# A new division of PSUM in windowed attention, and five units masked on TensorE

## The chip, the cores and the metric

One core of a Trainium2 chip runs the whole program. The metric is the device time of one execution in microseconds (us). Executions of the same kernel within one set of rounds here spread by 0.3 to 1.1%. One program is profiled once, so profiles of two kernels are two single executions, and the medians come from several.

## The reference

```python
# attention: B, H, S, D = 8, 8, 576, 64, window 64
scores = q @ k.T / sqrt(D)
scores = where(0 <= i - j < 64, scores, -1e9)
x = softmax(scores) @ v                  # heads side by side: (4608, 512)
# mixture of experts: 8 experts, F = 1024, one per token
logits = x @ w_gate
fresh = argmax(logits)
e = fresh where s == 0 or sigmoid(x @ w_local) < 0.5, else the previous token's e
out = softmax(logits)[e] * (relu(x @ w1[e]) @ w2[e])
```

## The kernel before

Attention takes the 4608 tokens as 9 blocks of 512 and the 8 heads as 4 pairs, which gives 36 units of one block and one pair. TensorE computes scores two units ahead, ScalarE takes exp, VectorE multiplies by a 0/1 mask, TensorE multiplies by the values, VectorE divides. In between, blocks 0 to 3 have their x turned (transposed) for the gates, blocks 4 to 8 get gates from turned values that are loaded, and VectorE works the first part of the router during blocks 4 to 7. After attention come the experts.

The kernel divides PSUM, the memory that TensorE's products land in, into 8 banks of 512 fp32 per partition. Before, two double banks hold scores and two double banks hold everything else: values, turns, gates, logits and the router's products.

```python
ps_s = tile_pool(name="at_ps_s", bufs=2, space=PSUM)          # (cut: contexts)
ps_x = [tile_pool(name=f"at_ps_x{i}", bufs=1, space=PSUM) for i in range(2)]

def bank():
    ps_x.reverse()
    return ps_x[0].tile([P, 2, SC], F32, name="xo")

def turn(sc, x, half):
    r = bank()
    for i in range(2):
        for c in range(4):
            nc.tensor.transpose(r[:, i, ...], x[:, c, 2 * half + i], ident)
    o = pp.tile([P, 2, SC], F32, name="p")
    nc.scalar.copy(o, r)

def scores(sc, hp):
    sp = ps_s.tile([P, 2, SC], F32, name="sp")
    ...                                    # 18 products of 64x64 with 64x128 or 64x64 (36 records in the trace)
    nc.scalar.activation(p, sp, Act.Exp, scale=DH ** -0.5)
    nc.vector.tensor_tensor(p, p, mask, op=Alu.mult)

def values(sc, hp, p, x, g):
    xo = bank()
    ...                                    # 16 products (32 records), then VectorE reads xo

for i, (sc, hp) in enumerate(units):
    ps[units[i + LEAD]] = scores(*units[i + LEAD])
    ...
    for _ in range(2 if sc else 4):
        next(moves, None)                  # shift copies of the next block's values, on ScalarE and GpSimd
    ...                                    # a turn, gates, logits or a copy of gates (spread)
    values(sc, hp, ps.pop((sc, hp)), x, g)
```

A shift copy makes a part of vb, a second arrangement of the next block's values; the gates' copy (spread) puts the turned gates beside the values.

## Time and profile before

| | before |
|---|---|
| time, median of 4 runs | 663.25 us (660.32 to 664.8) |
| profiled execution, span | 661.9 us |
| end of the last values product | 139.36 us |
| from there to the end (experts) | 522.5 us |
| TensorE's waits on ScalarE's turn copies | 2.4 + 0.8 us |
| TensorE's waits on the gates' copy and the logits | 5.3 + 1.9 us |

### The profile page before, as it was taken

The numbers are of one execution on the slowest core, as the hardware profiler recorded it, in microseconds if no ns is written. First come the engines' busy times: TensorE is split into PE (matmuls) and PEld (weight loads), VectorE is DVE, ScalarE is ACT, GpSimd is POOL, SyncE is SP. The second block draws the span as 40 slices with busy tenths as digits, with TensorE's granted clock in tenths as the row PEclk, the third lists the DMA queues.
The fourth block names the chain that finished last, engine by engine and source line by source line (L and its number), as shares of the span: only waits on it lengthen the run. The fifth ranks groups of instructions, "written<-read, shape, count | busy, mean of one in ns | idle before, by whom it ended". The sixth has DMA issues, their size and how long they took to land. (4 is left out here: it accounts for less than half of the span.)

```text
span 661.9 us, 15065 instructions
## 1 busy us (share of the span) xinstructions
PE 630.8 (95%) x6521; PEld 545.4 (82%) x6521; DVE 385.4 (58%) x693; ACT 177.7 (27%) x274; POOL 122.3 (18%) x128
## 2 busy tenths in 40 slices
PE   7888878999999999999999999999999999999996
PEld 7766666787677799989989998999799979997984
DVE  7665589774941268368528844863666366537410
ACT  4755645521111121212212230322131213211200
POOL 4311112311204111122113111311211120101011
PEclk9999998999999999999999999999999999999998
DMA  9989989999878967487468657755865586457540
GB/s 339 417 326 352 330 298 371 401 348 358 324 286 331 352 221 280 168 331 277 161 237 356 226 223 278 294 201 178 313 243 192 189 310 244 162 192 284 207 156 23
DMA packets 22479, 178.37 MB, mean 269 GB/s; under 512 B 3037, under 2 KB 4195, under 8 KB 11652
## 3 DMA queue, kind: packets, MB, share of 16 engines
q1 hardware_dynamic: 13588, 147.82, 59.3%
q0 software_dynamic: 8816, 29.50, 11.3%
q8 instruction: 53, 0.87, 0.5%
q14 instruction: 22, 0.18, 0.1%
HBM read 158.43 MB, written 19.40 MB: 269 GB/s over the span
## 5 line engine op out<-in xcount | busy, mean ns | idle before, releaser
L1185 POOL DMA_INDIRECT out_dram<-y,idx x36 | 38.2, 1061 | 301.1 <-DVE y L1164 141.9
L1203 PEld LDWEIGHTS hp<-xt,w 128*128 128x128 f32 (+1 forms) x1152 | 88.3, 168 | 3.6 <-issue 3.2
L1203 PE MATMUL hp<-xt,w 128*128 128x128 f32 (+1 forms) x1152 | 89.7, 252 | 0.0
L1112 PE MATMUL hp<-xs,ws 128*128 128x128 f32 x624 | 73.9, 275 | 0.0
L1112 PEld LDWEIGHTS hp<-xs,ws 128*128 128x128 f32 x624 | 71.8, 192 | 0.0
L1155 PE MATMUL hp<-ws,hs 128*128 128x256 f32 x312 | 71.6, 379 | 0.0
L1234 PE MATMUL yp<-w,h 128*128 128x512 f32 x160 | 71.0, 594 | 0.2 <-issue 0.2
L1036 POOL DMA_INDIRECT xg<-xs,idx x40 | 46.5, 1164 | 116.3 <-PE tp L1061 85.8
L1155 PEld LDWEIGHTS hp<-ws,hs 128*128 128x128 f32 x312 | 59.3, 190 | 8.1
L354 DVE TENSOR_TENSOR p<-p,mask 128x1024 f32<-128x1024 f32 x36 | 47.4, 1320 | 20.5 <-ACT p L351 20.2
L1234 PEld LDWEIGHTS yp<-w,h 128*128 128x128 f32 x160 | 29.5, 190 | 32.9 <-issue 32.1
L1123 DVE TENSOR_TENSOR h<-hp,keep 128x512 f32<-128x512 f32 x39 | 26.9, 691 | 49.0 <-PE hp L1112 48.0
L364 PE MATMUL xo<-vb,p 128*64 128x74 f32 (+1 forms) x576 | 44.4, 229 | 10.2 <-DVE va L304 5.3
L364 PEld LDWEIGHTS xo<-vb,p 128*64 128x64 f32 x576 | 38.9, 138 | 18.4 <-issue 8.6
L1112 PEld LDWEIGHTS hp<-xt,w 128*128 128x128 f32 x416 | 49.3, 192 | 3.4 <-issue 2.4
L1164 DVE SCALAR_TENSOR_TENSOR y<-hp,pw,kept 128x256 f32<-128x256 f32 x39 | 18.3, 482 | 56.2 <-issue 33.6
L1112 PE MATMUL hp<-xt,w 128*128 128x128 f32 x416 | 51.0, 276 | 0.0
L351 ACT ACTIVATE p<-sp 128x1024 f32<-128x1024 f32 x36 | 36.8, 1026 | 48.0 <-PE sp L335 43.1
L1155 PE MATMUL hp<-w,h 128*128 128x256 f32 x208 | 49.5, 381 | 0.0
L335 PE MATMUL sp<-w 64*64 64x128 f32 (+1 forms) x1296 | 43.1, 269 | 3.3 <-issue 2.0
L335 PEld LDWEIGHTS sp<-w 64*64 64x64 f32 x1296 | 37.4, 137 | 10.2 <-issue 6.9
L364 PE MATMUL xo<-va,p 128*64 128x74 f32 (+1 forms) x576 | 44.6, 230 | 1.0 <-issue 1.0
(268 smaller groups left out, 898.8 us busy)
## 6 DMA issues: line engine op xcount, KB each, us to landing
w<-in_w_dram SPq DMA_DIRECT2D x54, 2048.0 KB, 8.4
w<-in_kq_dram SPq DMA_DIRECT2D x17, 1024.0 KB, 10.5
xs<-x POOLq DMA_DIRECT2D x9, 1024.0 KB, 12.7
va<-in_v_dram SPq DMA_DIRECT2D x5, 1184.0 KB
vtt<-in_vt_dram SPq DMA_DIRECT2D x5, 1024.0 KB, 7.1
va<-in_v_dram SPq DMA_DIRECT2D x3, 1040.0 KB, 11.5
va<-in_v_dram SPq DMA_DIRECT2D x2, 520.0 KB, 10.3
w<-in_kq_dram SPq DMA_DIRECT2D x2, 512.0 KB
```

Of the source, the lines that this page charges most:

```text
L335: nc.tensor.matmul(sp[c * WIN:(c + 1) * WIN, j, a:b], lhsT=kt[h, hp, block * WIN:(block + 1) * WIN], rhs=qt[h, hp, a:b], start=True, stop= ...
L351: nc.scalar.activation(p, sp, Act.Exp, scale=DH ** -0.5)
L354: masked.append(nc.vector.tensor_tensor(p, p, m.to_broadcast([P, 2, SC]), op=Alu.mult))
L364: nc.tensor.matmul(xo[par * WIN:(par + 1) * WIN, j, s * VW:s * VW + n], lhsT=p[:, j, b * WIN:(b + 1) * WIN], rhs=w[:, s, 2 * hp + j, :n], ...
L1036: self.nc.gpsimd.indirect_dma_start(out=x, out_offset=None, in_=self.xs[:rows, :], in_offset=bass.IndirectOffsetOnAxis(ap=idx[:, s:s + 1], ...
L1112: nc.tensor.matmul(out[:, m, :], lhsT=a[:, kk, m * P:(m + 1) * P], rhs=b[:, kk, :], start=start and m + kk == 0, stop=stop and (m, kk) == ...
L1123: nc.vector.tensor_tensor(o, x, y, op=add)
L1155: nc.tensor.matmul(out, lhsT=a[:, m, :], rhs=b[:, m, :], start=start and m == 0, stop=stop and m == FK // 2 - 1, skip_group_check=True)
L1164: nc.vector.scalar_tensor_tensor(y[i][:, j * w:(j + 1) * w], x, pw[i], y2, Alu.mult, Alu.add)
L1185: self.nc.gpsimd.indirect_dma_start(out=self.out[:, :], out_offset=bass.IndirectOffsetOnAxis(ap=st["idx"][:, s:s + 1], axis=0), in_=y, in_ ...
L1203: nc.tensor.matmul(hp[a, i, :], lhsT=st["w1"][:, kk, m * P:(m + 1) * P][:, a], rhs=st["xt"][:, kk, :n], start=(kk == 0), stop=(kk == DK - 1))
L1234: nc.tensor.matmul(yp, lhsT=st["h"][:, m, :P], rhs=st["w2"][:, m, :], start=(m == 0), stop=(m == FK - 1))
```

## The change

The intent is to let no values product wait for a bank that gates or router steps hold. Scores get three single banks (so exp runs in two halves), values keep two double banks for themselves, and one single bank serves everything else. Five units at the time of the router leave VectorE's mask out: before the scores, TensorE adds -1e30 where the mask is 0 (an identity times a bias tile), so exp gives 0 there.

```diff
-    ps_s = ctx.enter_context(tc.tile_pool(name="at_ps_s", bufs=2, space=PSUM))
-    ps_x = [ctx.enter_context(tc.tile_pool(name=f"at_ps_x{i}", bufs=1, space=PSUM)) for i in range(2)]
+    ps_s = ctx.enter_context(tc.tile_pool(name="at_ps_s", bufs=3, space=PSUM))
+    ps_e = ctx.enter_context(tc.tile_pool(name="at_ps_e", bufs=1, space=PSUM))
+    ps_x = ctx.enter_context(tc.tile_pool(name="at_ps_x", bufs=2, space=PSUM))
     def bank():
-        ps_x.reverse()
-        return ps_x[0].tile([P, 2, SC], F32, name="xo")
+        return ps_e.tile([P, SC], F32, name="r")
...
+BIASED = [(4, 3), (5, 1), (5, 3), (6, 1), (6, 3)]
+    def build_bias():
+        colf = columns()                     # an iota and a cast in a buffer of the pool of p
+        ...                                  # four tensor_scalar into bias, then unit and never
...
     def scores(sc, hp):
-        sp = ps_s.tile([P, 2, SC], F32, name="sp")
+        sp = [ps_s.tile([P, SC], F32, name="sp") for _ in range(2)]
+        if biased:
+            ...
+            nc.tensor.matmul(sp[j][c * WIN:(c + 1) * WIN, a], lhsT=unit[h], rhs=x, start=not n, stop=False, ...)
...
-        nc.scalar.activation(p, sp, Act.Exp, scale=DH ** -0.5)
+        for j in range(2):
+            nc.scalar.activation(p[:, j], sp[j], Act.Exp, scale=DH ** -0.5)
+        if biased:
+            return p
...
-            if hp == 0:
-                turn(sc - 1, old, 1)         # 8 transposes into a double bank
+            if hp == 0:
+                turn(sc - 1, old, 2)         # 4 transposes, before values
...
+            if hp == 0:
+                turn(sc - 1, old, 3)         # 4 transposes, after values
...
+        sums = tl("sums", P, 2 * E * CMAX)[:, :2 * n * E]
+        vec.tensor_copy(sums, both)          # the router empties the single bank at once
```

The cuts hold the gates for 64 columns ahead of block 4 (now apart), a rule that router steps keep off the single bank while gates are in it, and tiles renamed. They also hold a change of TensorE's order: the first quarter of a turn moves up to unit 2 of its own block and the second to the end of unit 3, and the gates' transposes (logits) move from before the values of unit 2 to right after those of unit 1, so that one group of scores less stands between the gates product and them.

More of the change, by code (lines that the diff above doesn't have):

```diff
@@ L52 @@
 NEG = -1.0e9
+LOW = -1.0e30
 SC = 4 * P
@@ L187, in space @@
         return kp.tile([P, 4, H, width(sc)], F32, name=name, bufs=2 if name == "vb" else 3)
+    vhs = tp.tile([P, HP, SC], F32, name="vtt")[:, :, :WIN]
+    ahead = cp.tile([P, WIN], F32, name="ahead")
+    ahead_t = cp.tile([P, H, E + 1], F32, name="ahead_t")
     def load(sc, parts):
@@ L191, in load @@
             if part == "turned":
-                t = tp.tile([P, HP * (SC + WIN)], F32, name="vtt")
-                vts[sc] = main, ahead = t[:, :HP * SC], t[:, HP * SC:]
-                nc.sync.dma_start(out=main, in_=vt[GATED.index(sc)].rearrange("p h x -> p (h x)"))
-                if sc - 1 not in GATED:
-                    nc.sync.dma_start(out=ahead, in_=vh.rearrange("p h x -> p (h x)"))
+                vts[sc] = tp.tile([P, HP, SC], F32, name="vtt")
+                nc.sync.dma_start(out=vts[sc], in_=vt[GATED.index(sc)])
             elif isinstance(part, tuple):
@@ L222, in warm @@
         for _ in range(n):
-            nc.tensor.transpose(r[:, 0, :P], ident, ident)
+            nc.tensor.transpose(r[:, :P], ident, ident)
     warm(12)
@@ L233, in attention, with columns @@
     nc.vector.tensor_copy(rowf, row)
-    cols = pp.tile([P, 2, SC], F32, name="p").rearrange("p i (b q) -> p i b q", q=WIN)
-    col, colf = cols[:, 0].bitcast(I32), cols[:, 1]
-    nc.gpsimd.iota(col, pattern=[[0, KB], [1, WIN]], base=0, channel_multiplier=0)
-    nc.vector.tensor_copy(colf, col)
+    def columns():
+        cols = pp.tile([P, 2, SC], F32, name="p").rearrange("p i (b q) -> p i b q", q=WIN)
+        col, colf = cols[:, 0].bitcast(I32), cols[:, 1]
+        nc.gpsimd.iota(col, pattern=[[0, KB], [1, WIN]], base=0, channel_multiplier=0)
+        nc.vector.tensor_copy(colf, col)
+        return colf
+    colf = columns()
     masks = []
@@ L249, in build_mask, with turn @@
         masks.append(m.rearrange("p a b q -> p (a b q)"))
+    bias = cp.tile([P, 2, KB // 2, 2, WIN], BF16, name="bias")
+    never, unit = cp.tile([P, WIN], BF16, name="never"), cp.tile([P, WIN], BF16, name="unit")
+    def build_bias():
+        colf = columns()
+        for c in range(2):
+            for par in range(2):
+                nc.vector.tensor_scalar(bias[:, c, :, par, :], colf[:, :KB // 2], rowf, LOW,
+                                        Alu.is_lt if par == c else Alu.is_ge, Alu.mult)
+        nc.vector.tensor_scalar(unit, colf[:, 0], rowf, None, Alu.is_equal)
+        nc.vector.memset(never, LOW)
     build_mask(0)
     allr = cp.tile([P, NSC, HP, 2, 4], F32, name="allr")
-    def turn(sc, x, half):
+    def turn(sc, x, hp):
         r = bank()
-        for i in range(2):
-            for c in range(4):
-                nc.tensor.transpose(r[:, i, c * P:(c + 1) * P],
-                                    x[:, c, 2 * half + i].rearrange("p j d -> p (j d)"), ident)
-        o = pp.tile([P, 2, SC], F32, name="p")
-        nc.scalar.copy(o, r)
-        vts.setdefault(sc, []).append(o)
+        for c in range(4):
+            nc.tensor.transpose(r[:, c * P:(c + 1) * P], x[:, c, hp].rearrange("p j d -> p (j d)"), ident)
+        if hp % 2 == 0:
+            vts.setdefault(sc, []).append(pp.tile([P, 2, SC], F32, name="p"))
+        nc.scalar.copy(vts[sc][-1][:, hp % 2], r)
     def gates(sc):
         r = bank()
-        if sc in GATED:
-            main, ahead = (t.rearrange("p (h x) -> p h x", h=HP) for t in vts[sc])
+        gs = wk.tile([P, SC], F32, name="gs", bufs=1)
         for hp in range(HP):
@@ L272, in gates @@
             if sc not in GATED:
-                nc.tensor.matmul(r[h, 0, :], lhsT=wg[:, hp, :], rhs=vts[sc][hp // 2][:, hp % 2], start=True, stop=True)
+                nc.tensor.matmul(r[h, :], lhsT=wg[:, hp, :], rhs=vts[sc][hp // 2][:, hp % 2], start=True, stop=True)
                 continue
-            nc.tensor.matmul(r[h, 0, :], lhsT=wg2[:, hp, :], rhs=main[:, hp, :], start=True, stop=True)
-            if sc - 1 not in GATED:
-                nc.tensor.matmul(r[h, 1, :WIN], lhsT=wg2[:, hp, :], rhs=ahead[:, hp, :], start=True, stop=True)
@@ L278, in gates, with gates_ahead @@
-        n = SC + WIN if sc in GATED and sc - 1 not in GATED else SC
-        gs = wk.tile([P, SC + WIN], F32, name="gs", bufs=1)
-        nc.scalar.copy(gs[:, :n], r.rearrange("p i x -> p (i x)")[:, :n])
-        return r, gs
-    def back(r, gs):
+            nc.tensor.matmul(r[h, :], lhsT=wg2[:, hp, :], rhs=vts[sc][:, hp, :], start=True, stop=True)
+        nc.scalar.copy(gs, r)
+        return gs
+    def gates_ahead():
+        r = bank()
+        for hp in range(HP):
+            nc.tensor.matmul(r[hp * GW:(hp + 1) * GW, :WIN], lhsT=wg2[:, hp, :], rhs=vhs[:, hp, :],
+                             start=True, stop=True)
+        nc.scalar.copy(ahead, r[:, :WIN])
@@ L284, in back @@
+    def back(gs):
+        r = bank()
         for c in range(4):
-            nc.tensor.transpose(r[:, 1, c * P:(c + 1) * P], gs[:, c * P:(c + 1) * P], ident)
-        return r[:, 1, :]
+            nc.tensor.transpose(r[:, c * P:(c + 1) * P], gs[:, c * P:(c + 1) * P], ident)
+        return r
     def logits(sc, gated):
-        gt = back(*gated).rearrange("p (c h g) -> p c g h", c=4, h=HP)[:, :, :E + 1]
+        gt = back(gated).rearrange("p (c h g) -> p c g h", c=4, h=HP)[:, :, :E + 1]
         nc.vector.tensor_reduce(lt[:, 4 * sc:4 * sc + 4, :], gt, axis=AX.X, op=Alu.add)
@@ L293, in spread @@
     def spread(sc, gated):
-        r, gs = gated
-        gt = back(r, gs).rearrange("p (c h g) -> p c h g", c=4, h=H)[:, :, :, :E + 1]
+        gt = back(gated).rearrange("p (c h g) -> p c h g", c=4, h=H)[:, :, :, :E + 1]
         g = slice(VX, VW)
-        if sc - 1 not in GATED:
-            o = r[:WIN, 0, :P]
-            nc.tensor.transpose(o, gs[:, SC:], ident)
-            nc.scalar.copy(vbs[sc][WIN:, 0, :, g], o.rearrange("p (h g) -> p h g", h=H)[:, :, :E + 1])
+        if sc == GATED[0]:
+            nc.gpsimd.tensor_copy(vbs[sc][WIN:, 0, :, g], ahead_t[WIN:])
@@ L304, in spread, with back_ahead @@
         nc.vector.tensor_copy(vas[sc][:, :, :, g], gt)
+    def back_ahead():
+        o = bank()[:WIN, :P]
+        nc.tensor.transpose(o, ahead, ident)
+        nc.scalar.copy(ahead_t[WIN:], o.rearrange("p (h g) -> p h g", h=H)[:, :, :E + 1])
     def shift(sc):
@@ L330, in scores @@
         qt, kt = qts[sc], kts[sc]
-        sp = ps_s.tile([P, 2, SC], F32, name="sp")
+        sp = [ps_s.tile([P, SC], F32, name="sp") for _ in range(2)]
+        biased = (sc, hp) in BIASED
         def one(j, c, kt, block, a, b):
             h = slice(j * DH, (j + 1) * DH)
-            nc.tensor.matmul(sp[c * WIN:(c + 1) * WIN, j, a:b], lhsT=kt[h, hp, block * WIN:(block + 1) * WIN],
-                             rhs=qt[h, hp, a:b], start=True, stop=True)
+            nc.tensor.matmul(sp[j][c * WIN:(c + 1) * WIN, a:b], lhsT=kt[h, hp, block * WIN:(block + 1) * WIN],
+                             rhs=qt[h, hp, a:b], start=not biased, stop=True, skip_group_check=biased)
+        first = -sc * KB % SB
+        if biased:
+            for n in range(2):
+                for c in range(2):
+                    for j in range(2):
+                        h, a = slice(j * DH, (j + 1) * DH), slice(0, SC)
+                        x = bias[h, c].rearrange("p b i q -> p (b i q)")
+                        if n:
+                            if first >= KB or c == first % 2:
+                                continue
+                            a, x = slice(first * WIN, (first + 1) * WIN), never[h]
+                        nc.tensor.matmul(sp[j][c * WIN:(c + 1) * WIN, a], lhsT=unit[h], rhs=x, start=not n, stop=False,
+                                         skip_group_check=True)
         for s in range(5):
@@ L350, in scores @@
         p = pp.tile([P, 2, SC], F32, name="p")
-        nc.scalar.activation(p, sp, Act.Exp, scale=DH ** -0.5)
+        for j in range(2):
+            nc.scalar.activation(p[:, j], sp[j], Act.Exp, scale=DH ** -0.5)
+        if biased:
+            return p
         a = 0 if sc == KB else (MID[sc % 2] - sc) * WIN
@@ L358, in values @@
         va, vb, n = vas[sc], vbs[sc], width(sc)
-        xo = bank()
+        xo = ps_x.tile([P, 2, SC], F32, name="xo")
         for s in range(4):
@@ L389, in attention, with step @@
     side = None
-    pause = 0
-    def step():
-        nonlocal pause, side
+    pause, trip = 0, False
+    def step(free=True):
+        nonlocal pause, side, trip
         pause -= HALF
-        if side and pause <= 0.0:
+        if side and pause <= 0.0 and (free or not trip):
             w, trip = next(side, (0.0, None))
@@ L401, in step @@
                     ex.rows(ex.jobs[0], -1)
-    def psum():
-        return bank()[:, 0, :]
     for i, (sc, hp) in enumerate(units):
@@ L417, in attention @@
             next(moves, None) if moves else None
-        if hp == HP - 1:
-            if sc + 1 in GATED:
-                spread(sc + 1, gated)
-            if sc not in GATED:
-                turn(sc, x, 0)
-                old = x
-        elif sc and sc - 1 not in GATED:
+        if hp == 3 and sc + 1 in GATED:
+            spread(sc + 1, gated)
+        elif (sc, hp) == (1, 3):
+            gates_ahead()
+        elif (sc, hp) == (2, 3):
+            back_ahead()
+        elif hp == 2 and sc not in GATED:
+            turn(sc, x, 0)
+        elif sc and hp < 2 and sc - 1 not in GATED:
             if hp == 0:
-                turn(sc - 1, old, 1)
-            elif hp == 1:
+                turn(sc - 1, old, 2)
+            else:
                 turned = gates(sc - 1)
-            else:
-                logits(sc - 1, turned)
         if side is None and 4 * sc >= C1 and hp >= 2:
-            side = rt.first(psum)
-        step()
+            side = rt.first(bank)
+        step(not (hp == 3 and sc + 1 in GATED))
         values(sc, hp, ps.pop((sc, hp)), x, g)
@@ L441, in attention @@
             load(2, [pairs[0], whole, pairs[1]])
+            nc.sync.dma_start(out=vhs, in_=vh)
         if i == 2 * HP:
@@ L444, in attention @@
                 rt.prepare()
+                build_bias()
+        if sc not in GATED and hp == 3:
+            turn(sc, x, 1)
+            old = x
+        elif sc and hp < 2 and sc - 1 not in GATED:
+            if hp == 0:
+                turn(sc - 1, old, 3)
+            else:
+                logits(sc - 1, turned)
         if hp == 2 and sc + 1 in GATED:
@@ L456, in attention @@
             ex.jobs.append(ex.weights({}, -2))
-        step()
+        step(not (hp == 2 and sc + 1 in GATED))
         if hp == HP - 1:
@@ L469, in attention @@
     fl = allr.rearrange("p a b c d -> p (a b c d)")
-    f = wk.tile([P, NSC * 4 * H], F32, name="f", bufs=1)
+    f = wk.tile([P, SC], F32, name="gs", bufs=1)[:, :NSC * 4 * H]
     nc.vector.tensor_scalar(f, fl, 1e20, None, Alu.is_le)
@@ L778, in gate @@
         yield 0.6, True
-        both = psum()
-        pre, tot = both[:, :n * E], both[:, n * E:2 * n * E]
+        both = psum()[:, :2 * n * E]
         ohf = oh.rearrange("p c e -> p (c e)")
-        nc.tensor.matmul(tot, lhsT=self.ones, rhs=ohf, start=True, stop=True)
-        nc.tensor.matmul(pre, lhsT=self.tri, rhs=ohf, start=True, stop=True)
+        nc.tensor.matmul(both[:, n * E:], lhsT=self.ones, rhs=ohf, start=True, stop=True)
+        nc.tensor.matmul(both[:, :n * E], lhsT=self.tri, rhs=ohf, start=True, stop=True)
+        sums = tl("sums", P, 2 * E * CMAX)[:, :2 * n * E]
+        vec.tensor_copy(sums, both)
+        pre, tot = sums[:, :n * E], sums[:, n * E:]
         te = tl("te", P, E * CMAX)[:, :E * n].rearrange("p (e c) -> p e c", e=E)
```

## The prediction

> **What bounds the kernel now.** I read the table of windows first, because attention and the experts share one page and have different limits. Columns: stretch and length, busy us (instructions) of PE, PEld, DVE, ACT, POOL, then granted clock, DMA share and GB/s.
>
> ```profile
> 20.00:40.00 20.00, 17.11 (x387) 14.16 (x387) 11.92 (x17) 13.28 (x16) 6.15 (x7) 1.00 0.88 352
> ...
> 80.00:100.00 20.00, 15.46 (x372) 12.22 (x370) 17.93 (x62) 9.31 (x13) 2.99 (x3) 1.00 0.86 316
> 100.00:120.00 20.00, 16.79 (x415) 14.50 (x413) 19.51 (x55) 10.95 (x15) 6.67 (x6) 0.91 1.01 376
> ...
> 180.00:200.00 20.00, 20.00 (x122) 14.49 (x121) 8.56 (x6) 2.36 (x4) 3.04 (x2) 1.00 0.79 301
> ```
>
> Attention ends at about 139.4 us. From 160 us TensorE is busy in every microsecond, so the experts are TensorE's and the change barely touches them. I take them as a constant: whatever attention gains or loses moves the end of the kernel by as much. In attention no engine is full all the time. TensorE is 80 to 90% busy; VectorE is the tightest only from 80 to 120 us, where the first part of the router is worked in between. DMA is near its ceiling while it transfers, but the loads are issued two blocks ahead and TensorE's list of waits names none. So attention is an in-order chain on TensorE, broken by short waits. The list of TensorE's waits up to 142 us (sum, times, longest) has:
>
> ```profile
> PE xo L364 <- DVE va L304: 5.3, 3, 2.1
> ...
> PE xo L273 <- ACT p L262: 2.4, 4, 0.8
> PE sp L335 <- issue: 2.0, 3, 1.0
> ...
> PE xo L364 <- issue: 1.9, 2, 1.0
> PE xo L364 <- DVE lt L291: 1.9, 4, 0.5
> ```
>
> L364 is the values product, L304 copies the turned gates out of PSUM, L262 copies turned x out of PSUM, L273 is the gates product, L291 reduces the logits. Waits of a values product on L291 and most of those on L304 are waits for a bank, not for data, because all these share two double banks. One of the three on L304 (before TensorE at 104.9 us) is real data: the first values of a block read the copied gates. Removable bank waits are therefore about 1.2 + 2.1 + 1.9 = 5.2 us.
>
> **What the Trainium skill says.** "PSUM — Partial Sum Buffer", Specifications: 8 banks of 2 KiB, 512 fp32 each. Before uses 2x2 for scores and 2x2 for all else; after 3 + 2x2 + 1: nothing is added, the single bank is taken from the scores. The same page, Engine vs sequencer instructions, calls the queues of ScalarE and VectorE strict FIFO. The trace agrees: at 41.66 us the copy L262 runs only after two copies L311 and L314, though its input was ready at 39.94. "SBUF — State Buffer", in the section on its two separate sides, says that a VectorE operation with two SBUF inputs and a GpSimd operation that reads SBUF exclude each other. The trace is consistent: the mask product L354 that starts at 102.28 takes 2.19 us, against 1.22 usually, with a GpSimd copy of 1.31 us beginning at 102.08.
>
> **The change, part by part.**
>
> *Exp in two halves.* L262, a ScalarE copy, takes 1012 ns for 128x1024 and L280 586 ns for 128x512, so a second instruction costs 2 x 586 - 1012 = 160 ns. For 36 units that is 5.8 us of ScalarE work. ScalarE is at most 13.3 of 20 busy, so this is mostly beside other work; it lengthens the queue ahead of a copy by 0.15 us. Scores now need the first half of the previous unit's exp done. In steady state values (about 1.1 us) stand between, which covers it. At the start, the second unit's scores wait for the first half of the first exp, an estimated 0.9 us, of which I keep 0.5 because the first scores of block 1 stand at 16.05 us anyway (I take that wait for the landing of their load).
>
> *One bank for everything else.* The order of instructions shows, in the first unit of blocks 1 to 4: scores, turn (4 transposes), values, turn (4), scores, gates, values. The second turn must wait until ScalarE has copied the first out of the only bank. The ScalarE timeline at block 2 before (start, duration):
>
> ```profile
> 39.00 1.03 ACT L351 ACTIVATE p<-sp 128x1024 f32<-128x1024 f32 x1 [1.17 <-PE sp L335]
> 40.05 0.62 ACT L311 COPY vb<-va 64x520 f32<-64x520 f32 x1
> 40.58 1.05 ACT L314 COPY vb<-va 64x1040 f32<-64x1040 f32 x1
> 41.66 1.01 ACT L262 COPY p<-xo 128x1024 f32<-128x1024 f32 x1
> 42.57 1.03 ACT L351 ACTIVATE p<-sp 128x1024 f32<-128x1024 f32 x1
> ```
>
> The reader is to see that two shift copies stand between exp and the turn's copy; that order stays. Put on the same clock: scores end at 38.9, first turn 39.5, values 40.6; ScalarE exp to 40.2, copies to 41.85, the turn's copy to 42.4. The second turn thus waits 42.5 - 40.6 = 1.9 us, and nothing on TensorE can pass it. Before, scores filled this time and only 0.66 to 0.80 us was left. The net loss is about 1.2 us, four times (blocks 1 to 4): +4.8. The gates' later transposes wait for L344 and the copy of the gates, an estimated 0.5 us, as the values waited 0.47 for the logits before: nil. In the second half of block 3 the 1.2 us wait on L304 passes from the values to the turn behind them: nil. Part of the new wait hides the ~1 us stalls that the profile calls issue (0.4 to 1.0 us, inside a group of scores or values, five between 26 and 80 us, perhaps instruction fetch): an estimated -2.
>
> *Bias tiles.* Worked once in block 2 on VectorE: a cast (L237 took 0.83), four 128x256 operations (about 0.27 each, scaled from 0.445 for L245's 64x512), two small ones: 2.2 us, and 0.6 of iota on GpSimd. VectorE was already full there with the router's preparation (42 to 43.7 us). I charge 0.5 on the path through the logits.
>
> *Five units without the mask product.* L354 costs 1.22 us unblocked and 2.19 once: 5 x 1.22 + 0.97 = 7.1 us off VectorE between roughly 75 and 112 us, less one added copy of 128x224 from PSUM (an estimated 0.35). On TensorE each gains four bf16 products of 512 columns (two more of 64 columns in some), on four quarters of the array; 8 records of 128x512 f32 took 1.06 us in L275, so I estimate 0.35 to 0.4 us a unit, 2 us in all. From the first scores of (4,2) at 70.1 us to the end of values (7,0) at 119.6 the old kernel takes 49.4 us; TensorE's own work there is about 37 us. Walking the new order unit by unit with the durations above leaves waits of 1.9 (turn, already counted net), 1.3 (carry of the router's scan), 0.6 (one-hot), 1.3 (values of (6,0) on the gates, still data), 1.0 (values (6,2) on VectorE's reading of a value bank), 0.3. Old waits in this stretch sum to about 8.9. So 8.9 - 0.7 (turn) - 4.5 = 3.7 saved, less 2 of bias products: about -2. VectorE stops being full, but the one-bank chain and the router's dependent steps keep most of the gaps.
>
> *Last two blocks.* The 0.95 us wait of values on L889 at 122 us goes (router's table has its own bank): -1.
>
> Sum: +0.5 + 4.8 - 2 + 0.5 - 2 - 1 = +0.8 us by the walk.
>
> **The rivals.** *The bank division pays as meant.* All 5.3 + 1.9 us of bank waits and the VectorE congestion vanish and the turn's wait is small: for it speaks the 95 to 100% VectorE load from 95 to 115 us and that the five units lie just where the L304 copies were late; it would give 8 to 10 us, about 654. Against it stand ScalarE's queue above and that half of the L304 wait is data. *The single bank becomes the bound.* Every gates, turn and router step queues on it, each evacuation behind other VectorE or ScalarE work, losing 1.9 us in blocks 1 to 4 and 1 us in blocks 5 to 8 at several places: about 669. Against: scores or values stand between most users, 1.1 us each. *DMA hides any gain.* 316 to 376 GB/s in 80 to 120 us against a best window of about 426; there is room for some 10% before loads bind, so a gain of 5 us would come through. This would leave 660 to 663.
>
> **Range and chances.** The walk gives 663.8; the list of removable waits and the relief of VectorE argue for more gain than a walk with every instruction in its worst place shows, so I lean to the rival that it pays and put 661.8. Both rivals' ends plus the 0.3% spread of runs give 654 to 669. 2% is 13 us: faster would need more than half of all TensorE idle time in attention (some 22 us) to go, slower a new stall in every unit.
>
> **What would show it.** Right: a wait of the second turn on ScalarE's copy of the first of about 1.9 us, four times; no wait of values on L291 or, before block 4's last values, on the gates' copy; VectorE clearly below 18 of 20 in 90 to 110 us; attention ending within 5 us of 139.4; the stretch from there to the end unchanged at about 522 us. Wrong: the four turn waits are absent or under 1 us (then the change is a gain of some 5 us); or scores wait on exp in steady state; or the experts' part changes length.

## More of the kernel before

The orders of TensorE, ScalarE and the DMA queue are as written; VectorE's is made by a scheduler when the program is built.

The page's group of the mask product is one to keep. Its columns are line, engine, operation, names, shapes and count, then busy us and mean ns of one, then idle time of the engine before it and what ended it:

```profile
L354 DVE TENSOR_TENSOR p<-p,mask 128x1024 f32<-128x1024 f32 x36 | 47.4, 1320 | 20.5 <-ACT p L351 20.2
L351 ACT ACTIVATE p<-sp 128x1024 f32<-128x1024 f32 x36 | 36.8, 1026 | 48.0 <-PE sp L335 43.1
```

The mask costs VectorE 47.4 us in all, more than exp costs ScalarE. The reader should not take that for the path: in attention, VectorE is nearly full only between 80 and 120 us.

## The result, and the profile after

| | before | after |
|---|---|---|
| time, median of 4 runs | 663.25 us | 670.08 us (667.89 to 670.49) |
| the same, in a later set of rounds | 663.0 us (11 runs) | 667.77 us (6 runs) |
| ratio, 95% interval | | 1.0101 (1.006 to 1.0143), later 1.0074 (1.0058 to 1.009) |
| profiled span | 661.9 us | 668.2 us |
| end of the last values product | 139.36 us | 145.96 us |
| from there to the end | 522.5 us | 522.2 us |

A ratio is the mean time of one kernel's runs over the mean of the other's in the same rounds, so it is not quite the ratio of the medians. The change makes the kernel slower, by 0.7 to 1%. All of it is in attention, which ends 6.6 us later; the experts' stretch is unchanged. The table of windows after, with the columns as before:

```profile
20.00:40.00 20.00, 14.83 (x370) 12.12 (x362) 10.33 (x16) 12.44 (x22) 4.64 (x4) 1.00 0.91 352
...
80.00:100.00 20.00, 16.95 (x406) 13.14 (x410) 12.21 (x42) 11.99 (x22) 2.98 (x3) 1.00 0.86 309
100.00:120.00 20.00, 15.24 (x377) 11.95 (x367) 19.46 (x68) 9.39 (x17) 3.18 (x3) 1.00 1.00 367
...
180.00:200.00 20.00, 20.00 (x138) 15.99 (x137) 15.48 (x12) 2.95 (x5) 5.87 (x3) 1.00 0.88 339
```

TensorE is busy for 14.83 of the 20 us after 20 us, against 17.11 before: the loss begins long before the router. VectorE is relieved from 80 to 100 us (17.93 became 12.21) but is as full as before from 100 to 120 (19.51 and 19.46). TensorE's waits up to 147 us (sum, times, longest):

```profile
PE r L280 <- ACT p L283: 8.1, 5, 1.9
PE sp L362 <- issue: 4.2, 2, 2.2
PE r L309 <- ACT gs L295: 2.9, 4, 1.7
...
PE xo L408 <- DVE va L325: 2.8, 1, 2.8
PE xo L408 <- DVE x L418: 1.7, 2, 1.4
PE xo L408 <- issue: 1.5, 2, 1.2
PE r L280 <- DVE va L325: 1.2, 1, 1.2
```

L280 is the turn, L283 its copy on ScalarE, L309 the transposes of the gates, L295 the gates' copy, L408 values, L325 the copy of the gates that was L304, and L362 the scores. The wait at the top did not exist in this form before. ScalarE's timeline at block 2, the place that the prediction showed:

```profile
41.96 1.08 ACT L393 ACTIVATE p<-sp 128x512 f32<-128x512 f32 x2 [0.49 <-PE sp L362]
43.07 0.62 ACT L337 COPY vb<-va 64x520 f32<-64x520 f32 x1
43.59 1.05 ACT L340 COPY vb<-va 64x1040 f32<-64x1040 f32 x1
44.67 0.59 ACT L283 COPY p<-r 128x512 f32<-128x512 f32 x1
46.00 0.59 ACT L283 COPY p<-r 128x512 f32<-128x512 f32 x1 [0.75 <-PE r L280]
```

and TensorE's at the same place (start, duration, what it waited for):

```profile
45.31 0.66 PE L280 MATMUL r<-ident,x 128*128 128x128 f32 x4 [1.75 <-ACT p L283]
```

The first turn's transposes were done at 42.5 us, but its copy stands behind exp and two shift copies and ends at 45.26. Only then may the second turn start. Values ended at 43.56; TensorE works in the order written, and the turn is next.

I added the waits of the two lists by kind, to see whether they give the 6.6 us:

| kind | before | after | difference |
|---|---|---|---|
| turns and first gates on ScalarE's turn copies | 3.2 | 8.1 | +4.9 |
| values on the logits; gates' transposes on the gates' copy | 1.9 | 2.9 | +1.0 |
| issue (stalls inside a group) | 4.4 | 5.7 | +1.3 |
| values on VectorE's reading of their bank (x and allr) | 0.8 | 2.0 | +1.2 |
| on the gates' copy into the values' tile | 5.3 | 4.7 | -0.6 |
| router's products and gates on each other | 3.3 | 1.2 | -2.1 |
| scores at the start | 1.2 | 0.5 | -0.7 |
| bias products (5 x 0.24, below) | 0 | 1.2 | +1.2 |

The sum is 6.2 us, close to 6.6. The windows agree: up to the last values product TensorE's idle time rose from 23.4 to 27.7 us, and its busy time from 116.0 to 118.25, of which the bias products are 1.2.

### The profile page after: what moved, and what is told of

It reads as the page before. It is cut to its first block, busy times and chain, and to the rows that moved or that the text cites. A ratio compares the mean times of both kernels' runs of the same rounds, so it can differ in the third digit from the quotient of the medians.

```text
span 668.2 us, 15153 instructions
## 1 busy us (share of the span) xinstructions
PE 632.5 (95%) x6551; PEld 544.5 (81%) x6551; DVE 382.2 (57%) x697; ACT 181.3 (27%) x319; POOL 128.9 (19%) x130
## 5 line engine op out<-in xcount | busy, mean ns | idle before, releaser
L1240 POOL DMA_INDIRECT out_dram<-y,idx x36 | 40.9, 1135 | 303.2 <-DVE y L1219 141.1
L1091 POOL DMA_INDIRECT xg<-xs,idx x40 | 48.3, 1208 | 110.7 <-PE tp L1116 81.0
L398 DVE TENSOR_TENSOR p<-p,mask 128x1024 f32<-128x1024 f32 x31 | 39.0, 1258 | 33.4 <-ACT p L393 33.2
L393 ACT ACTIVATE p<-sp 128x512 f32<-128x512 f32 x72 | 39.1, 595 | 43.3 <-PE sp L362 40.7
L408 PE MATMUL xo<-vb,p 128*64 128x74 f32 (+1 forms) x576 | 44.8, 231 | 3.2 <-DVE x L418 1.7
L362 PEld LDWEIGHTS sp<-w 64*64 64x64 f32 x1296 | 37.7, 137 | 12.2 <-issue 9.1
L408 PE MATMUL xo<-va,p 128*64 128x74 f32 (+1 forms) x576 | 44.7, 231 | 3.1 <-DVE va L325 2.8
L362 PE MATMUL sp<-w 64*64 64x128 f32 (+1 forms) x1296 | 43.0, 269 | 4.8 <-issue 4.2
L408 PEld LDWEIGHTS xo<-vb,p 128*64 128x64 f32 x576 | 39.2, 139 | 9.7 <-issue 5.4
```

Source lines behind the costliest of these rows:

```text
L362: nc.tensor.matmul(sp[j][c * WIN:(c + 1) * WIN, a:b], lhsT=kt[h, hp, block * WIN:(block + 1) * WIN], rhs=qt[h, hp, a:b], start=not biased, ...
L393: nc.scalar.activation(p[:, j], sp[j], Act.Exp, scale=DH ** -0.5)
L398: masked.append(nc.vector.tensor_tensor(p, p, m.to_broadcast([P, 2, SC]), op=Alu.mult))
L408: nc.tensor.matmul(xo[par * WIN:(par + 1) * WIN, j, s * VW:s * VW + n], lhsT=p[:, j, b * WIN:(b + 1) * WIN], rhs=w[:, s, 2 * hp + j, :n], ...
L1091: self.nc.gpsimd.indirect_dma_start(out=x, out_offset=None, in_=self.xs[:rows, :], in_offset=bass.IndirectOffsetOnAxis(ap=idx[:, s:s + 1], ...
L1240: self.nc.gpsimd.indirect_dma_start(out=self.out[:, :], out_offset=bass.IndirectOffsetOnAxis(ap=st["idx"][:, s:s + 1], axis=0), in_=y, in_ ...
```

## The experiments

Theory T: the loss is the second turn, which waits for the only free bank behind ScalarE's shift copies. Rival B: the bias parts cost more than the masks they save. Rival F: stalls that the profile calls issue make the difference. The runs were in three sets, each on a chip of its own with its own 11 runs of the kernel before; each kernel has 6 runs. So a ratio is the number to compare between sets. No run took the exp in halves or TensorE's new order alone.

| run | median us | ratio to before, 95% interval |
|---|---|---|
| no_bias | 669.23 | 1.0079 (1.0053 to 1.0106) |
| copy_first | 664.24 | 1.0015 (0.9983 to 1.0048) |
| own_columns | 667.5 | 1.0059 (1.0026 to 1.0092) |
| both | 664.44 | 1.0013 (0.9984 to 1.0043) |
| before_bias | 663.19 | 1.0002 (0.9987 to 1.0018) |
| before_copy_first | 661.7 | 0.9984 (0.9964 to 1.0004) |
| before_both | 663.05 | 0.9996 (0.9977 to 1.0016) |
| after_again | 667.77 | 1.0074 (1.0058 to 1.009) |
| spread_copies | 661.39 | 0.9956 (0.9934 to 0.9977) |
| spread_va | 661.54 | 0.9977 (0.9957 to 0.9997) |
| before_va | 664.07 | 1.0015 (0.998 to 1.0049) |
| before_va_only | 663.79 | 1.0017 (0.9991 to 1.0044) |

**no_bias**: the new division alone.

```diff
-BIASED = [(4, 3), (5, 1), (5, 3), (6, 1), (6, 3)]
+BIASED = []
-                build_bias()
```

> The new division of PSUM alone: no biased units, and the bias tiles are not built. Theory T (the loss is the second turn waiting for the only bank behind ScalarE's shift copies): the turn waits stay at about 8 us in all; 1.2 us of TensorE work and 1.2 us of the late exp in block 2 go, but VectorE gets 5 mask products of 1.22 us back, so 668 to 672 us. Rival B (the bias parts are the loss): about 664, level with before. Rival F (late instruction fetches, which fall where they fall): anything from 666 to 672 with the issue stalls moved.

Measured 1.0079, the same as the whole change in after_again (1.0074). The turn waits are 8.1 us in its profile too. Rival B falls: without the bias parts the loss is all there. Its list of TensorE's waits has:

```profile
PE r L280 <- ACT p L283: 8.1, 5, 1.9
PE xo L408 <- DVE va L325: 5.4, 2, 3.6
```

The second line was 2.8 with the bias parts; with the turns and the router that wait on the same copy, 7.7 us against 4.7. So the bias parts do take about 3 us of waits away, and they cost about 2.5 (1.2 of products, 1.3 of the late exp, below): too near to each other for the times to show. The issue stalls are only 1.8 us in this profile and the loss is there all the same, which speaks against rival F too.

**copy_first**: the changed kernel with only the order on ScalarE altered.

```diff
-        for _ in range(2 if sc else 4):
-            next(moves, None) if moves else None
+        turning = hp == 0 and sc and sc - 1 not in GATED
+        if not turning:
+            for _ in range(2 if sc else 4):
+                next(moves, None) if moves else None
...
                 turn(sc - 1, old, 3)
+                for _ in range(2):
+                    next(moves, None) if moves else None
```

> The changed kernel with only ScalarE's order altered: in the first unit of blocks 1 to 4 the two shift copies come after both turn copies. Theory T: turn waits fall from 8.1 us to under 3, time 664 to 666 us (4 to 6 less than the change). Rival B and rival F: no change from the turn, 669 to 670.

Measured 1.0015, level with before. No instruction was taken away; two copies per block moved behind two others. Its list of TensorE's waits has:

```profile
PE r L309 <- ACT gs L295: 6.1, 4, 1.7
...
PE r L280 <- ACT p L283: 1.1, 1, 1.1
```

The turns' wait fell from 8.1 to 1.1 us. But the gates' transposes now wait 6.1 us, against 2.9: the shift copies stand ahead of exp and of the gates' copy instead. So 7.0 us went and 3.2 came back, which fits a gain of about 4 us (0.6% of 663) over after_again. Theory T stands, and in a wider form: whichever copy out of the single bank stands behind the shift copies is the one that TensorE waits for. The two waits differ in kind. The second turn needs only the bank; the gates' transposes also read what the gates' copy wrote, so they would wait for it with any number of banks, and they stand nearer behind it than before.

**own_columns**: the column index of the bias tiles in a tile of its own.

```diff
-        colf = columns()
+        coli, colf = cp.tile([P, 1, WIN], I32, name="coli"), cp.tile([P, 1, WIN], F32, name="colo")
+        nc.gpsimd.iota(coli, pattern=[[0, 1], [1, WIN]], base=0, channel_multiplier=0)
+        nc.vector.tensor_copy(colf, coli)
...                                           # the bias operations read it broadcast
```

> The changed kernel with only the bias tiles' column index in a tile of its own (64 columns) and not in one of the five buffers of p. The 1.26 us that exp waited for VectorE's bias tiles in block 2 and half of the cast's time go: 668.5 to 669.5 us, with the turn waits untouched at 8 us. Theory T and rival B agree here; if it gives 3 us or more, rival B is the larger part.

Measured 1.0059, a little below the change (1.0074 in other rounds), and a median of 667.5 us, 1 us below the range expected; the intervals overlap, so the time alone doesn't settle it. The profile does for the wait. In the changed kernel ScalarE had:

```profile
48.37 1.08 ACT L393 ACTIVATE p<-sp 128x512 f32<-128x512 f32 x2 [1.78 <-DVE unit L270]
```

Exp stood 1.78 us idle until VectorE had built the bias tiles, and the longest wait of the gates' transposes was 1.7 us; here this exp stands idle for 0.49 us, for its scores, and that longest wait is 0.4 us. **both** joins the two edits.

> Both edits together. Theory T: the gains add, 663 to 665 us, about level with before, since the remaining losses (bias products 1.2 us, data waits on the gates) balance the masks saved. Rival B: 668.

Measured 1.0013, no different from copy_first: the gains did not add. In both runs the same 6.1 us of gates' transposes remain. In copy_first exp of block 2 ran at 45.26 with no idle time before it, so the wait on the bias tiles was gone there already.

**before_bias**: the five biased units in the kernel before, PSUM untouched (the same lines as in the change, with the tile of own_columns).

> The kernel before, its PSUM untouched, with only the five units masked by TensorE (bias tiles from a tile of its own). Theory T: the masks taken off VectorE shorten the late copies of the gates; 1.2 us of bias products are added; 660 to 662 us, 1 to 3 less than before. Rival B (bias parts are the loss): 666 to 669.

Measured 1.0002: a miss. No loss, so rival B falls a second time, but no gain either. TensorE's wait on the gates' copy did not shrink:

```profile
PE xo L396 <- DVE va L320: 6.4, 3, 3.5
```

It was 5.3 with at most 2.1. The VectorE timeline shows why: where the mask product was, the scheduler puts more router steps ahead of the gates' copy, and two of them fall on a GpSimd copy. In this kernel, at 99.77 us:

```profile
99.77 1.10 DVE L872 TENSOR_SCALAR lo_i<-plc_i 128x14 int32<-128x14 int32 x1
100.91 1.08 DVE L873 TENSOR_SCALAR plc_i<-plc_i 128x14 int32<-128x14 int32 x1
```

The same operations take 0.17 and at most 0.18 us in the kernel after. GpSimd copies of 1.17 us began at 99.67 and 100.78, a moment before each. The Trainium skill, "SBUF — State Buffer", Who interferes with whom, says that tensor_scalar may enter a mode that uses the port pair shared with GpSimd, and that whoever issues first holds the pair for the whole instruction. The trace is consistent with it, though no run here took the GpSimd copies away. (In the kernel before, it is the mask product of 2.19 us that stands there, as the prediction shows.) The changed kernel has the same at 107.31 us, where a 1x6 operation takes 1.14 us under a GpSimd copy that began at 107.22, and values of block 6 then wait 2.8 us for the gates' copy. So part of what the masks gave back was probably lost to this.

**before_copy_first**: in the kernel before, the shift copies after the turn's copy.

```diff
+        turning = hp == 0 and sc and sc - 1 not in GATED
+        if not turning:
+            for _ in range(2 if sc else 4): ...
...
                 turn(sc - 1, old, 1)
+                for _ in range(2):
+                    next(moves, None) if moves else None
```

> The kernel before with only ScalarE's shift copies put after the turn's copy in the first unit of blocks 1 to 4. The gates' product no longer waits for the turn's copy, 2.4 us in all, and the 0.8 us at 23.7 us may stay: 660.5 to 662 us by theory T, which says such waits are on the path. If they are hidden elsewhere, 663.

Measured 0.9984 (0.9964 to 1.0004), about 1 us where I expected 1 to 2.5; the interval just includes no change. The 2.4 us of waits of the gates are gone from its list, but the issue stalls sum to 7.5 us in its profile, against 4.4. **before_both** adds the biased units.

> The kernel before with both: five biased units and the copies in the better order. If the two gains add: 658 to 661 us, better than both kernels of the case.

Measured 0.9996: a miss, no gain. Values still wait 6.1 us for the gates' copy in its profile.

**after_again**: the changed kernel unaltered.

> The changed kernel unaltered, for its spread beside the others and to see whether the issue stalls stand at the same matmuls: 669 to 671 us; by rival F the stalls stand at the same positions (multiples of 127 matmuls) but differ in length.

Median 667.77, below the expected 669 to 671. Its issue stalls sum to 4.2 us, against 5.7 in the first profile and 4.4 in the kernel before. Over all profiles they sum to between 1.8 us (no_bias) and 9.4 (before_va), so a difference of 1 or 2 us between two profiles says little. Their positions are the point. I counted the TensorE records up to a stall. Before (window from 0 to the stall, then TensorE busy us with matmuls and weight loads counted in brackets):

```profile
0.00:19.70 19.70, 15.79 (x349) 14.51 (x349) 14.13 (x26) 8.24 (x9) 8.13 (x23) 1.00 0.92 351
0.00:26.60 26.60, 21.66 (x475) 19.54 (x476) 19.52 (x32) 14.37 (x16) 10.44 (x25) 1.00 0.94 370
0.00:33.50 33.50, 27.34 (x602) 23.73 (x603) 23.25 (x37) 18.90 (x21) 12.67 (x27) 1.00 0.96 379
```

and the first stall of the changed kernel in its second profile:

```profile
0.00:20.90 20.90, 16.46 (x349) 14.61 (x350) 14.38 (x26) 8.87 (x14) 10.67 (x24) 1.00 0.92 353
```

The stalls lie 126 and 127 matmul records apart, with as many weight loads: 252 to 254 instructions. Of the seven stalls of the kernel before, six lie at such steps (the others at records 856, 984 and 1492); the one of 0.35 us at record 2409 does not. And both kernels stall at matmul 349, though they have other instructions there. The Trainium skill, "Runtime: NRT & Kernel Launch", Instruction fetch mechanics, says that TensorE's instructions come in blocks of 256 by DMA, and calls the cost of a boundary mostly hidden. The spacing is near that, the cost is not: 0.2 to 2.2 us at these. The same boundary cost 2.18 us in one execution of the changed kernel and 0.50 in the other, so rival F can explain 1 to 2 us of spread between executions; a steady loss is not seen. That a busy DMA makes the fetch late is my reading; no run took the traffic away.

**spread_copies**: the changed kernel with the tile of own_columns and one shift copy at a time: one after the turns, one after the gates' copy, the rest in the third unit.

```diff
-        for _ in range(2 if sc else 4):
-            next(moves, None) if moves else None
+        turning = sc and hp < 2 and sc - 1 not in GATED
+        if not turning:
+            for _ in range(2 if sc else 4):
+                next(moves, None) if moves else None
...
             else:
                 logits(sc - 1, turned)
+            next(moves, None) if moves else None
```

> The changed kernel with the column index in its own tile and ScalarE's shift copies spread in blocks 1 to 4: one after the turns, one after the gates' copy, the last in the third unit. In the run with both turns first, the wait moved from the turns (8.1 to 1.1 us) to the gates' transposes (2.9 to 6.1 us), because the shift copies now stood ahead of the gates' copy. If theory T is right in full (the single bank held behind ScalarE's shift copies, wherever they stand), both waits are small now, turns near 1 and gates under 2.5 us, and the time is 659 to 661.5 us, below before. If other work fills the gap, 663 to 664.

Measured 661.39 us and 0.9956 (0.9934 to 0.9977): faster than both kernels, by some 3 us against before and 8 to 10 against the change (1.0101 or 1.0074 less 0.9956 is 1.2 to 1.5% of 663). The nearest kernel is both (1.0013), which has the same tile of own_columns and differs only in where the shift copies stand: spreading them is worth about 4 us more. In its list, where L282 is the turn and L296 the gates:

```profile
PE xo L410 <- DVE va L327: 2.8, 1, 2.8
...
PE r L282 <- ACT p L285: 1.1, 1, 1.1
...
PE r L296 <- ACT p L285: 0.8, 1, 0.8
```

No wait of the gates' transposes on the gates' copy is in the list any more. Theory T holds: with ScalarE emptying the single bank in time, the loss is gone. That the bank then costs nothing is not shown: turns still wait 1.1 us for ScalarE and 1.2 us for the gates' copy in this profile. Nor is it shown that the new division beats the old one, as no run spread the copies in the kernel before; the nearest, before_copy_first, has 0.9984, and the intervals overlap.

**spread_va**: the same, with the gates' copy (L327) on ScalarE. **before_va** and **before_va_only**: the same move in the kernel before, with and without the better order of the shift copies.

```diff
-        nc.vector.tensor_copy(vas[sc][:, :, :, g], gt)
+        nc.scalar.copy(vas[sc][:, :, :, g], gt)
```

> The same, and the copy of the turned gates into the values' tile goes from VectorE to ScalarE, behind its two sisters. The waits of TensorE on that copy (2.8 + 1.2 + 0.7 us in the changed kernel, called waits on the gates' copy) go, ScalarE gets 0.45 us a block: 655 to 658 us, below both kernels. If VectorE's order only moves the wait to its reading of the values' bank, 659 to 661.

> The kernel before with the shift copies after the turn's copy and the gates' copy on ScalarE. Of 5.3 us of waits of values on the gates' copy 3.5 to 4.5 go: 657 to 659 us. Does the old division of PSUM, so mended, stand level with the new one mended in the same way? By the view that the single bank costs nothing once ScalarE frees it in time, within 2 us of the run before this one.

> The kernel before with only the gates' copy moved to ScalarE: 658.5 to 660.5 us; waits of values on the gates' copy at most 1.5 us.

Measured 0.9977, 1.0015 and 1.0017: three misses. The waits aimed at did shrink: values no longer wait 2.8 us for the gates' copy in spread_va, and in before_va_only the 5.3 us became 2.5. But values then wait for VectorE's reading of their bank, 2.4 us once in spread_va and 1.8 us in two waits in before_va_only, and the issue stalls are longer, 6.6 us in the profile of spread_va and 9.4 in that of before_va, against 4.4 before. Why the stalls sum to more in these runs is open. So this part of the waits was not worth its length. My reading is that VectorE is the limit there, and where it is not waited for at one place it is at the next. The test in the expectation of before_va failed narrowly too: it lies 2.5 us above spread_va, not within 2, though the intervals touch and the order of the shift copies is not the same in the two.

## Why the prediction was wrong

I put 661.8 us in a range of 654 to 669; the change measured 670.08 and 667.77 later. The mechanism was right in blocks 1 to 4, where the rival that I called "the single bank becomes the bound: about 669" happened as said. Its other half, 1 us at several places in blocks 5 to 8, shows no loss on balance: waits on the gates' copy were 4.7 us against 5.3, and those of the router 1.2 against 3.3. So the nearness of its 669 to the time is partly luck. What failed is the step that took 2 us off for stalls hidden in the new wait, and then the lean 2 us below the sum; the turn's wait itself was sized well.

- *The turn's wait, +4.8.* Right. Predicted 1.9 us, four times, net of what was there; measured 1.46, 1.75, 1.87 and 1.83 in blocks 1 to 4, and 1.14 at the turn before it in block 1, which was not forecast. With what was there before taken off (2.4 and 0.8), the four give +4.5 and the fifth +0.3. The run copy_first took the loss back by order alone.
- *Exp in halves.* Smaller than thought: two halves took 1.08 us together against 1.03 for the whole, where I charged 0.16. Scores waited on exp for 0.3 us in all (0.8 in after_again), at the start; with the wait for a load, the scores' waits there fell from 1.2 to 0.5 us, where I charged +0.5.
- *"Part of the new wait hides the ~1 us stalls ... an estimated -2."* This step failed. The stalls were 4.4 us before and 5.7 (again: 4.2) after. They come at fixed counts of instructions, in the middle of scores or values, so a wait elsewhere did not take them up. The term was +1.3 or -0.2 in place of -2. With one profile of the kernel before, its exact size is open.
- *Bias tiles, +0.5.* Mis-sized: exp of block 2 was held back, not only the logits, and the gates' transposes waited 1.68 us in place of about 0.4, so +1.3.
- *Five units without the mask, -2 from the first scores of (4,2) to values (7,0).* Not settled: 47.1 us before and 46.4 after, from scores to scores, and this includes 1.1 us more of turn wait, so -1.8 as it stands. But TensorE's granted clock fell to 0.50 at 106 to 108 us in the profile of before, and there one group of scores took 1.98 us in place of 1.12 and two of values 1.81 and 1.37 in place of 1.26: 1.5 us that belong to the clock and not to the masks. In the profile after, this stretch has the full clock and such a dip comes at 131 to 133 us. So somewhere between 0.3 and 1.8 us were gained. The bias products cost 0.24 us a unit (scores follow each other by 1.29 us with them and by 1.05 without), where I estimated 0.4. In the kernel before they gained nothing (before_bias), and taking them out of the changed kernel lost nothing (no_bias).
- *Last two blocks, -1.* Wrong in this execution: 22.1 us became 23.2, with one issue stall of 1.99 us among them, and with the dip of the clock, where one group of values took 2.25 us in place of 1.26. The wait that I said would go is gone from the list.
- *The lean.* The walk gave 663.8, and I went 2 us below it because the list of removable waits (5.2 us) looked larger. That was the wrong direction: the 1.9 us of values on the logits came back as 2.9 of the gates' transposes, and the 5.3 on the gates' copy stayed at 4.7, part of it now in front of a turn and a router product. With the measured -0.2 to +1.3 for the stalls and +1.3 for the bias tiles, the walk gives 663.8 + 1.8 to 3.3 + 0.8 = 666.4 to 667.9. The first rounds lie 2 us above that, the later ones at it; the difference between those two sets is not explained. (The 1.2 us too much charged at the start, the gain of the five units and the last two blocks are left out here; together they would move this by something between -1 and +3 us.)
- *The experts are a constant.* Right: 522.5 and 522.2 us. The first product of the experts now waits 1.4 us for VectorE's last reading of x, as its bank was a values bank before; the 1.1 us that another product waited there before is gone in exchange.
- *The signs.* Of what was to show it right, the four turn waits came, no values waited on the logits, VectorE was busy 16.7 of 20 us from 90 to 110 (19.3 before), and the experts kept their length. Attention ended 6.6 us later, not within 5.

## What to carry to other kernels

In this kernel a bank that several users share one after another cost what its slowest emptying cost, and on an engine that works in order that was decided by what else stood in the queue ahead of the copy. So when buffers become fewer, look at the emptying engine's order first: here moving two copies behind two others was worth 4 us, and spreading them (with the bias index in its own tile) 8 to 10, with no copy removed. And relief of a full engine can be worth nothing, as in before_bias, if a scheduler fills the room with work that again comes before what the path needs. Look at the granted clock, too, before you compare a stretch of two profiles.

## What the Trainium skill lacked or had wrong

- "Runtime: NRT & Kernel Launch", Instruction fetch mechanics, calls crossing a block mostly hidden. Here, where the stalls lie 252 to 254 instructions apart, TensorE stood 0.2 to 2.2 us at a boundary in the profiles of the change and of before, and such stalls sum to 4.2 to 5.7 us over attention. The page gives no such cost; the cause is read from the spacing.
- "PSUM — Partial Sum Buffer" tells how to keep engines apart in a bank, but not what sharing one costs. With ScalarE's queue ahead of the copy, one bank reused at once held TensorE for 1.1 to 1.9 us each time, 8.1 us in all.
- "SBUF — State Buffer", Who interferes with whom, was consistent with the trace. It has no size for small operations: one of 0.17 us took 1.10 us under a GpSimd copy of 1.17 us.
